# GpSimd in source order beside the attention, ScalarE and TensorE behind it, full rows in the middle slot, and a thinner last side slot

## The chip, the cores and the metric

The kernel runs on one core of a Trainium2 chip. Its engines are TensorE (PE in the profile, with its weight loads as PEld), VectorE (DVE), ScalarE (ACT), GpSimd (POOL) and SyncE (SP), whose queue issues most transfers; the indirect transfers (gathers and scatters by row index) are issued by GpSimd. Each engine takes its instructions strictly in the order in which the program has them, so one that waits holds everything behind it on that engine. The metric is the device time of one execution in microseconds.

## The reference

Attention over 8 batches, 8 heads, 576 positions and 64 dimensions, with a softmax that keeps only scores within `tau` of the row's maximum, and behind it a mixture of eight experts, of which each token takes one:

```
scores = scale * np.matmul(q, k.transpose(0, 1, 3, 2))
thresh = np.max(scores, axis=-1, keepdims=True) - tau
scores = np.where(scores >= thresh, scores, -1e9)
attn = softmax(scores);  x = attn @ v          # 4608 tokens of 512
logits = x @ w_gate + modality_bias[modality_id]
e_idx = np.argmax(logits, axis=1)              # top 1 of 8 experts
for e in range(E):
    h = np.maximum(x[mask] @ w1[e], 0.0)       # 512 -> 1024
    out[mask] = gate_w[mask, None] * (h @ w2[e])
```

All of it is in fp32. The kernel reaches that with operands split in two, a rounded high part and the rest as a low part (names with `h` and `l`), and three matmuls in place of one.

## The kernel before, in words

**The attention loop.** 32 pairs of heads, nine query tiles each, make 288 steps. A step does the scores (L369), their row maximum (VectorE, L386), the exponential (ScalarE, L392), mask and sum (VectorE, L404), transposes (L420) and the product with v (L458). Beside the steps of one pair the next is prepared by `prep_steps`: PE transposes k and q, ScalarE evacuates them as `str` (the last 64 positions) and `st` (the rest; L314), GpSimd splits them into high and low parts (`split_pool`, L282 and L283) `nk`, `qb` and `nq`, and SP then moves the parts to where the matmuls want them: `km<-nk` (L320) and `q<-nq` (L323), four transfers each. The first score tile of a pair reads `nk` and `qb`, the next ones `km` and `q`.

**The experts.** As soon as a batch is done, its tokens are routed. `route_a` and `route_b` rank them by expert (matmuls with the names `oh` and `ltri`), `posi` (L611) holds the rows, and five scatters (L617) write the table `tab` of token numbers, sorted by expert. A "slot" is a block of tokens of one expert (512, or 256 for the first two side slots). Seven side slots run beside the attention, one for each batch from the second on. A slot reads its piece of the table (`tb`, SP, L735), gathers its tokens (`xg`, GpSimd, L747, one for 128 tokens), transposes them (L761), and does both layers in pieces of three matmuls (L805 and L832). The weights arrive as `raw` (SP, L771 and L775; four buffers) and GpSimd splits them into `w1h`, `w1l`, `w2h`, `w2l` (L790, L792). The result `y` (VectorE, L845) is scattered to the output (GpSimd, L847). What a slot has to do besides matmuls are events with a due time in steps; its pieces wait in a queue, and each step takes some of them, spread so that the last side slot is done after `last` steps.

**The tail.** Behind the loop come the last batch's routing (`finish`, at XF = 301.5 steps), what is left of the last side slot, and from F0 = XF + 9.5 on the four slots that are always there (two of 512 tokens, one of 320, one of 256), whose high weight parts ScalarE splits off (L788). Conditional slots follow, which this data does not need.

**What sets the order.** `run_events` runs the events by their due time, which gives the order of the source. Engines named in `tc.manual_schedule(engines=...)` keep that order; the instructions of the others are ordered by a scheduler that works from modelled durations. Before, the loop has this for PE alone, and the tail for no engine.

Of the kernel before, what the change touches and what calls it, by code (L numbers as in the profile page):

```python
# [11 lines left out]
F32 = mybir.dt.float32  # L12
# [3 lines left out]
U32 = mybir.dt.uint32  # L16
# [3 lines left out]
ET = mybir.EngineType  # L20
# [9 lines left out]
def tile_attn_moe(  # L30
# [11 lines left out]
    out: bass.AP,  # L42
):

    C = {'prep': [0, 1, 2], 'tr0': 6, 'pv0': 7, 'tr1': 12, 'sums': 13, 'pv1': 13, 'x': 14, 'gate': [15, 16, 17, 18], 'route': 18, 'routeb': 21, 'E0': 28, 'L0': 4, 'pick': -14, 'vld': 6, 'qkld': -3, 'pre': 2.5, 'wl': 3.5, 'rows': -11, 'gat': [-9.5, -8.5, -5, -4], 'xt': [-6, -5, -2, -1], 'lc': 21, 't3': 84, 'neg': 1.0, 'draw': [2, 2, 2, 2, 1, 2, 2, 1, 2], 'last': 36, 'te': 8, 'warm': 24,
         'wS': [-6, -4.7, -3.4, 3, 12.5, 14, 15.5, 21.5, 4.2, 5.4, 6.6, 7.5, 22.7, 23.8, 24.9, 25.8],
         'wL': [-5.5, -4, -2.5, 2.7, 12, 13.3, 14.6, 21, 3.8, 4.9, 6, 7.1, 15.8, 22.2, 23.4, 24.6], 'ask': 4, 'exp': -12.5, 'two': 98, 'early': []}
    nc = tc.nc
# [2 lines left out]
    DM = H * D  # L51
    DF = w1.shape[2]
    N = B * S
    P = 128
# [8 lines left out]
    W = 512  # L63
# [498 lines left out]


    prev_scatter = []

    def route_a(b):
        lg = state.pop(("lg", b))
# [20 lines left out]
    def route_b(b):  # L588
        l, oh = state.pop(("route", b))
        shp = [P, NT, NE]  # L590

        rk = tbank()
        rkv = rk[:, 0:(NT + 1) * NE].rearrange("p (t e) -> p t e", e=NE)
        mm(rkv, ltri, oh, True, False)
        for t in range(NT):
            mm(rkv[:, t + 1:NT + 1, :], ones_bf, oh[:, t:t + 1, :].to_broadcast([P, NT - t, NE]),
               False, t == NT - 1)

        nc.scalar.activation(out=l, in_=l, func=AF.Exp)
        pos = small.tile([P, NT + 1, NE], F32, name="pos", bufs=1)  # L600
        nc.vector.tensor_tensor(out=pos, in0=rkv, in1=base.unsqueeze(1).to_broadcast([P, NT + 1, NE]),
                                op=ALU.add)
        nc.vector.tensor_copy(out=base, in_=pos[:, NT, :])
        nc.vector.tensor_tensor(out=pos[:, 0:NT, :], in0=pos[:, 0:NT, :],
                                in1=creg.unsqueeze(1).to_broadcast(shp), op=ALU.add)
        nc.vector.tensor_tensor(out=pos[:, 0:NT, :], in0=pos[:, 0:NT, :], in1=oh[:, 0:NT, :], op=ALU.mult)
        posi = small.tile([P, NT], I32, name="posi")
        posf = small.tile([P, NT], F32, name="posf", bufs=1)
        nc.vector.tensor_reduce(out=posf, in_=pos[:, 0:NT, :], axis=AX.X, op=ALU.add)
        nc.vector.memset(posf[0:P - R, NC:NT], float(TROWS))  # L610
        nc.vector.tensor_copy(out=posi, in_=posf)  # L611
        gs = small.tile([P, NT], F32, name="gs", bufs=1)
        nc.vector.tensor_reduce(out=gs, in_=l, axis=AX.X, op=ALU.add)
        nc.vector.tensor_scalar(out=gs, in0=gs, scalar1=1e-9, scalar2=None, op0=ALU.add)
        nc.vector.reciprocal(out=pay[:, b, :, 1].bitcast(F32), in_=gs)
        for t in range(NT):
            i = _inst(nc.gpsimd.indirect_dma_start(  # L617
                out=tab, out_offset=bass.IndirectOffsetOnAxis(ap=posi[:, t:t + 1].bitcast(U32), axis=0),
                in_=pay[:, b, t, :], in_offset=None, bounds_check=TROWS - 1, oob_is_err=False))
            for o in prev_scatter:  # L620
                tc.declare_no_dep(i, o, reason="every token has a row of its own")
            prev_scatter.append(i)
# [91 lines left out]
    def slot(where, group, nrow, WT=W, wq=lambda: wp, nbuf=(4, 3, 5), lo_eng=None, xq=None):  # L714
# [3 lines left out]
        box = {}  # L718
# [3 lines left out]
        def TP(t):  # L722

            return min(P, WT - t * P)
# [17 lines left out]
        def gather(t):  # L742
            def f():
                xg = xt_pool().tile([P, DM], F32, name="xg", bufs=nx[1])
                box[("xg", t)] = xg

                nc.gpsimd.indirect_dma_start(  # L747
                    out=xg[0:TP(t)], out_offset=None, in_=xs[0:nrow, :],
                    in_offset=bass.IndirectOffsetOnAxis(ap=box["tb"][0:TP(t), t, 0:1].bitcast(U32), axis=0),
                    bounds_check=nrow - 1, oob_is_err=False)  # L750
            return f

# [68 lines left out]
        def l2(g, t, z):  # L821
            def f():
                if z == 0:
                    box["ps"] = group()
                nt = TP(t)
                ps = box["ps"]
                ts = slice(t * P, (t + 1) * P)
                f_ = g * F2 + z
                hh, hl = box[("h", f_)]
                wh, wl = box[("w", 2, f_)]  # L830
                for y, (h, w) in enumerate(((hh, wh), (hh, wl), (hl, wh))):
                    nc.tensor.matmul(out=ps, lhsT=h[:, ts], rhs=w, start=(z == 0 and y == 0),  # L832
                                     stop=(z == F2 - 1 and y == 2))
                if z < F2 - 1:
                    return
                let_go(ps)
                ps = ps[0:nt]
                tb = box["tb"][0:nt]
                if g == 0:
                    y0 = xp.tile([P, DM], F32, name="y0", bufs=W // P)[0:nt]  # L840
                    nc.scalar.activation(out=y0, in_=ps, func=AF.Copy, scale=tb[:, t, 1:2].bitcast(F32))
                    box[("y0", t)] = y0
                    return
                y = xp.tile([P, DM], F32, name="y", bufs=2)[0:nt]
                nc.vector.scalar_tensor_tensor(out=y, in0=ps, scalar=tb[:, t, 1:2].bitcast(F32),  # L845
                                               in1=box.pop(("y0", t)), op0=ALU.mult, op1=ALU.add)
                i = _inst(nc.gpsimd.indirect_dma_start(  # L847
                    out=out, out_offset=bass.IndirectOffsetOnAxis(ap=tb[:, t, 0:1].bitcast(U32), axis=0),
                    in_=y, in_offset=None, bounds_check=N - 1, oob_is_err=False))
                for o in prev_out:  # L850
                    tc.declare_no_dep(i, o, reason="every token has a row of its own")
                prev_out.append(i)
            return f
# [48 lines left out]
    def at(t, f):  # L902
        events.setdefault(t, []).append(f)
# [118 lines left out]
        clear(fin["xp"], 4)  # L1022

    XF = NSTEP - NI + C['routeb'] + 1.5
    F0 = XF + 9.5
    at(XF, finish)

    def ask():
# [8 lines left out]
    def run_events(lo, hi):  # L1037
        while True:
            ts = [x for x in events if lo <= x < hi]
            if not ts:  # L1040
                return
            t = min(ts)
            for f in events.pop(t):
                f()

    LAG = 2
    with tc.manual_schedule(engines={ET.PE}):

        ps = tbank()
        for _ in range(C['warm']):  # L1050
# [1 line left out]
        prep_first(0)  # L1052
        for n in range(NSTEP + LAG):
            m = draw[n]
            if n == C['lc']:
                late_constants()
            if n == C['lc'] + 6:
# [32 lines left out]
            at(n + 0.01 * z, f)  # L1090
    for z, f in enumerate(work_q):
        at(NSTEP + LAG + z / 2, f)
    run_events(0, 10 ** 9)

    def more(cnt, j, z):
        if j < MAXN[z]:
# [39 lines left out]
```

## Time and profile before

| what | value |
|---|---|
| time, median of 3 runs | 1117.74 us (1115.88 to 1118.3) |
| time of the profiled execution | 1116.18 us |
| span of the profiled execution | 1114.5 us |
| PE busy | 1029.7 us, 92% of the span |
| VectorE, ScalarE, GpSimd busy | 725.7, 641.9, 537.9 us |
| mean granted TensorE clock | 0.976 of full speed |

In a group of the page stand the line, the engine, the operation, what it writes and reads, its count, then its busy time and the mean of one in ns, and the idle time of the engine just ahead of it with what ended most of it. In a row of an engine's timeline stand the start, the length, the instruction, and in brackets the idle time before it and what ended that. SPq is SP's queue, where a row is the issuing and not the transfer. A row of stretches gives the window, its length, then busy time and count for PE, PEld, DVE, ACT and POOL, the granted clock, the share of DMA, and GB/s.

### The profile page before, as it was taken

To read this page: it belongs to the slowest core of one execution; us is meant where nothing else is said; L and a number is where in the kernel's file an instruction comes from. 1 tells how busy PE (TensorE), PEld (TensorE's weight loads), DVE (VectorE), ACT (ScalarE), POOL (GpSimd) and SP (SyncE) were. 2 spreads that over 40 slices of the span, in tenths; PEclk is the share of its full clock that TensorE was granted. 3 is DMA by queue.
4 is the path that set the end of the run, shared out by engine and by line. 5 is a ranking of instruction groups with operands and counts; after the bars stand their busy time and mean duration, and the time that the engine had idled before them with its cause. 6 is when DMAs were issued, how large, how long until landed. Compare 5 with 4: busy or idle time off the path is not lost.

```text
span 1114.5 us, 20778 instructions
## 1 busy us (share of the span) xinstructions
PE 1029.7 (92%) x6683; PEld 809.9 (73%) x6683; DVE 725.7 (65%) x1773; ACT 641.9 (58%) x1474; POOL 537.9 (48%) x727
## 2 busy tenths in 40 slices
PE   7799869989798989999999999999999997999993
PEld 6676647777676767787777777777767775788883
DVE  6788857787568756876676766776677645243441
ACT  5687657666565656666666666566656523434440
POOL 2232345464655563665355644565265546442440
PEclk8999989999899999999999999999999999999997
DMA  5656557656666757476635763676465214644330
GB/s 123 140 136 160 124 128 184 165 110 165 165 161 130 180 129 184 102 202 162 168 82 141 197 161 91 148 206 147 107 141 152 97 39 134 216 145 131 131 99 21
DMA packets 212646, 156.06 MB, mean 140 GB/s; under 512 B 100782, under 2 KB 172462, under 8 KB 212528
## 3 DMA queue, kind: packets, MB, share of 16 engines
q1 hardware_dynamic: 205392, 135.72, 49.1%
q0 software_dynamic: 7136, 18.92, 5.2%
q8 instruction: 55, 0.90, 0.3%
q14 instruction: 63, 0.52, 0.1%
HBM read 84.12 MB, written 19.35 MB: 93 GB/s over the span
## 4 chain that ended last, share of the span: by engine, by line
PE 57%; DVE 3%; issue 2%; DMA 2%; ACT 1%; POOL 1%; another core or an unknown queue 0%; POOLq 0%; ACTq 0%; SPq 0%
PE bk L458 8%; PE bk L832 8%; PE bk L805 8%; PE s L369 8%; PE pm L832 7%; PE pm L805 6%; PE bk L420 6%; PE bk L761 1%; PE bk L311 1%; DVE pr L404 1%; PE bk L449 1%; DVE nm L386 1%; ACT e L392 1%; DMA xg<-xs,tb 1%; PE bk L507 1%
## 5 line engine op out<-in xcount | busy, mean ns | idle before, releaser
L386 DVE TENSOR_REDUCE nm<-s 128x1 f32<-128x576 f32 x288 | 216.9, 754 | 135.1 <-PE s L369 125.2
L392 ACT ACTIVATE e<-s,nm 128x576 f32<-128x576 f32 x288 | 215.0, 747 | 113.8 <-DVE nm L386 107.2
L404 DVE SCALAR_TENSOR_TENSOR pr<-s,nm,e 128x576 f32<-128x576 f32 x288 | 231.5, 815 | 75.1 <-ACT e L392 67.4
L369 PE MATMUL s<-km,q 128*128 128x288 f32 x1024 | 202.3, 320 | 41.1 <-DMA q<-nq 17.2
L431 ACT COPY ptm<-bk 128x512 f32<-128x512 f32 x256 | 149.3, 584 | 78.4 <-PE bk L420 66.4
L369 PEld LDWEIGHTS s<-km,q 128*128 128x128 f32 x1024 | 148.5, 192 | 62.1 <-issue 33.5
L420 PE MATMUL bk<-ident,pr 128*128 128x128 f32 x1152 | 175.8, 276 | 3.9 <-ACT ptm L431 2.0
L420 PEld LDWEIGHTS bk<-ident,pr 128*128 128x128 f32 x1152 | 143.6, 142 | 27.9 <-DVE hl L816 3.0
L458 PE MATMUL bk<-ptm,v_m 128*64 128x320 f32 (+1 forms) x1024 | 144.5, 420 | 0.1
L792 POOL TENSOR_TENSOR w2l<-raw,w2h 128x512 fp32r<-128x512 f32 x88 | 113.7, 1299 | 30.9 <-ACT w2h L788 26.7
L458 PEld LDWEIGHTS bk<-ptm,v_m 128*64 128x64 f32 x1024 | 67.6, 139 | 50.1 <-issue 10.3
L790 POOL CAST w2h<-raw 128x512 fp32r<-128x512 f32 x56 | 34.2, 613 | 140.1 <-DMA raw<-in_moe_w_dram 71.1
L433 ACT COPY rp<-pr 128x64 f32<-128x64 f32 x256 | 59.3, 248 | 56.5 <-DVE pr L404 47.0
L805 PE MATMUL bk<-xh,w1h 128*128 128x512 f32 (+1 forms) x212 | 85.5, 403 | 1.1 <-ACT xh L272 0.9
L805 PE MATMUL bk<-xl,w1h 128*128 128x512 f32 (+1 forms) x212 | 77.3, 365 | 1.9 <-DVE xl L273 1.9
L805 PE MATMUL bk<-xh,w1l 128*128 128x512 f32 (+1 forms) x212 | 76.9, 363 | 0.0
L747 POOL DMA_INDIRECT xg<-xs,tb x37 | 38.2, 1034 | 79.3 <-DMA tb<-tab 55.6
L832 PE MATMUL bk<-w2h,hh 128*128 128x512 f32 x176 | 75.7, 430 | 0.0
L847 POOL DMA_INDIRECT out_dram<-y,tb x37 | 38.6, 1042 | 74.4 <-DVE y L845 53.2
L792 POOL TENSOR_TENSOR w1l<-raw,w1h 128x512 fp32r<-128x512 f32 x56 | 71.8, 1285 | 2.9
L832 PE MATMUL bk<-w2h,hl 128*128 128x512 f32 x176 | 69.4, 394 | 0.0
L792 DVE TENSOR_TENSOR w1l<-raw,w1h 128x512 fp32r<-128x512 f32 x32 | 29.0, 908 | 61.5 <-ACT w1h L788 52.0
(205 smaller groups left out, 2006.7 us busy)
## 6 DMA issues: line engine op xcount, KB each, us to landing
raw<-in_moe_w_dram SPq DMA_DIRECT2D x176, 256.0 KB
q<-nq SPq DMA_DIRECT2D x124, 256.0 KB
km<-nk SPq DMA_DIRECT2D x124, 144.0 KB
v_m<-in_v_dram SPq DMA_DIRECT2D x32, 256.0 KB
xs<-xr SPq DMA_DIRECT2D x32, 256.0 KB
k_m<-in_k_dram SPq DMA_DIRECT2D x62, 128.0 KB
q_m<-in_q_dram SPq DMA_DIRECT2D x62, 128.0 KB
vr<-in_v_dram SPq DMA_DIRECT2D x64, 16.0 KB
```

The lines of the kernel that those rows point to most:

```text
L369: nc.tensor.matmul(out=sps[:, hf, 0:SH], lhsT=a, rhs=x, start=(z == 0), stop=(z == len(passes) - 1))
L386: in_line(nc.vector.tensor_reduce(out=nm[:, 0:1], in_=sv, axis=AX.XY, op=ALU.max, negate=True), two)
L392: nc.scalar.activation(out=e, in_=sv, func=AF.Exp, bias=nm[:, 0:1])
L404: in_line(nc.vector.scalar_tensor_tensor(out=pr.rearrange("p (a x) -> p a x", a=2), in0=s2[n % 2][:, :, 0:SH], scalar=nm[:, 1:2], in1=e, o ...
L420: nc.tensor.transpose(out=ps[:, kc * P:(kc + 1) * P], in_=pr[:, kc * P:(kc + 1) * P], identity=ident)
L431: nc.scalar.copy(out=ptm[:, s, :, (c % 2) * P:(c % 2 + 1) * P], in_=pv)
L433: nc.scalar.copy(out=rp[:, i, :], in_=pr[:, SA:S])
L458: nc.tensor.matmul(out=o, lhsT=lhsT, rhs=rhs, start=start, stop=stop, skip_group_check=True)
L792: eng.tensor_tensor(out=lo, in0=raw, in1=hi.bitcast(F32), op=ALU.subtract)
L805: nc.tensor.matmul(out=ps[:, 0:WT], lhsT=a[:, cs], rhs=x[:, c, :], start=(c == 0 and z == 0), stop=(c == KC - 1 and z == 2))
L832: nc.tensor.matmul(out=ps, lhsT=h[:, ts], rhs=w, start=(z == 0 and y == 0), stop=(z == F2 - 1 and y == 2))
L847: i = _inst(nc.gpsimd.indirect_dma_start(out=out, out_offset=bass.IndirectOffsetOnAxis(ap=tb[:, t, 0:1].bitcast(U32), axis=0), in_=y, in_o ...
```

## The change

Three edits, and two numbers that go with them.

- **Order.** In the loop GpSimd keeps the order of the source too, beside PE. In the tail ScalarE and PE keep it, where the scheduler ordered all engines.
- **Scatter.** The five table scatters are no longer issued inside `route_b` but by an event one step later (`'sc': 1`, function `scatter`), which puts them at a later place in the source order.
- **Full rows.** In the middle slot of 320 tokens the third tile has 64 tokens. Its gather, ScalarE's copy, VectorE's sum and the scatter now take all 128 partitions; the index rows behind the 64 point past the end and are dropped by the bounds check.
- **Numbers.** `last` goes from 36 to 50, so the last side slot's pieces are spread thinner and 57 of them are left for the tail where 53 were. F0 goes from XF + 9.5 to XF + 14.

```
-  'last': 36, 'te': 8, 'warm': 24,
+  'last': 50, 'te': 8, 'f0': 14, 'sc': 1, 'warm': 24,
...
+    step = [0]
...
         nc.vector.reciprocal(out=pay[:, b, :, 1].bitcast(F32), in_=gs)
+        at(step[0] + C['sc'], lambda: scatter(b, posi))
+
+    def scatter(b, posi):
         for t in range(NT):
             i = _inst(nc.gpsimd.indirect_dma_start(
                 out=tab, out_offset=bass.IndirectOffsetOnAxis(ap=posi[:, t:t + 1].bitcast(U32), axis=0),
...
-                    out=xg[0:TP(t)], out_offset=None, in_=xs[0:nrow, :],
-                    in_offset=bass.IndirectOffsetOnAxis(ap=box["tb"][0:TP(t), t, 0:1].bitcast(U32), axis=0),
+                    out=xg, out_offset=None, in_=xs[0:nrow, :],
+                    in_offset=bass.IndirectOffsetOnAxis(ap=box["tb"][:, t, 0:1].bitcast(U32), axis=0),
...
-                ps = ps[0:nt]
-                tb = box["tb"][0:nt]
+                tb = box["tb"]
...
-                    y0 = xp.tile([P, DM], F32, name="y0", bufs=W // P)[0:nt]
+                    y0 = xp.tile([P, DM], F32, name="y0", bufs=W // P)
...
-                y = xp.tile([P, DM], F32, name="y", bufs=2)[0:nt]
+                y = xp.tile([P, DM], F32, name="y", bufs=2)
...
-    F0 = XF + 9.5
+    F0 = XF + C['f0']
...
-    with tc.manual_schedule(engines={ET.PE}):
+    with tc.manual_schedule(engines={ET.PE, ET.Pool}):
...
+            step[0] = n
...
-    run_events(0, 10 ** 9)
+    with tc.manual_schedule(engines={ET.Activation, ET.PE}):
+        run_events(0, 10 ** 9)
```

Line numbers from L617 on grow by 4 and those behind the slot's second layer by 2 or 3: L747 is L751 after the change, L792 is L796, L847 is L849.

**The order on GpSimd, first side slot.** Behind the first table scatter of the run, before the change, from the split of the next pair's keys (`nk_152<-st`) to that of its queries (`nq<-st`). The slot's first gather stands ahead of these rows, right behind the five scatters.

```order
L282 CAST nk_152<-st 128x512
L790 CAST w1h<-raw 128x512
L283 TENSOR_TENSOR nk_152<-st,nk_152 128x512
L792 TENSOR_TENSOR w1l<-raw,w1h 128x512
L790 CAST w1h<-raw 128x512
L747 DMA xg<-xs,tb 128x512
L792 TENSOR_TENSOR w1l<-raw,w1h 128x512
L790 CAST w1h<-raw 128x512
L792 TENSOR_TENSOR w1l<-raw,w1h 128x512
L282 CAST nq<-st 128x512
L283 TENSOR_TENSOR nq<-st,nq 128x512
```

The same place after the change:

```order
L282 CAST nk_152<-st 128x512
L283 TENSOR_TENSOR nk_152<-st,nk_152 128x512
L282 CAST nq<-st 128x512
L283 TENSOR_TENSOR nq<-st,nq 128x512
L794 CAST w1h<-raw 128x512
L796 TENSOR_TENSOR w1l<-raw,w1h 128x512
L751 DMA xg<-xs,tb 128x512
L794 CAST w1h<-raw 128x512
L796 TENSOR_TENSOR w1l<-raw,w1h 128x512
L751 DMA xg<-xs,tb 128x512
```

The queries' split moved from behind both gathers and three weight splits to ahead of all of them.

**The order on SP, second side slot.** SP's row in the second side slot, some 140 us later, up to the transfers of the queries of one pair (`q_147`), before (an ISA row is a register instruction that goes with the load behind it):

```order
L775 DMA raw<-in_moe_w_dram 128x512
L771 ISA
L771 DMA raw<-in_moe_w_dram 128x4x128
L771 ISA
L771 DMA raw<-in_moe_w_dram 128x4x128
L113 DMA q_r<-in_q_dram 64x2x64
L113 DMA k_r<-in_k_dram 64x2x64
L771 ISA
L771 DMA raw<-in_moe_w_dram 128x4x128
L115 DMA k_m<-in_k_dram 128x4x64 x2
L320 DMA km_149<-nk_151 64x576 x4
L323 DMA q_147<-nq 64x2x512 x4
```

SP's row up to the same transfers after:

```order
L779 DMA raw<-in_moe_w_dram 128x512
L113 DMA q_r<-in_q_dram 64x2x64
L113 DMA k_r<-in_k_dram 64x2x64
L115 DMA k_m<-in_k_dram 128x4x64 x2
L320 DMA km_149<-nk_151 64x576 x4
L323 DMA q_147<-nq 64x2x512 x4
L779 ISA
L779 DMA raw<-in_moe_w_dram 128x512
```

The loads of w1 that stood ahead of `km` and `q` come later now, though SP's order is the scheduler's in both.

**The order on GpSimd at the handover.** Around the last batch's five scatters, before (`w2h`, `w2l` and the last `w1h`, `w1l` belong to the last side slot, the four gathers to the first slot of the tail):

```order
L790 CAST w2h<-raw 128x512
L792 TENSOR_TENSOR w2l<-raw,w2h 128x512
L790 CAST w2h<-raw 128x512 x2
L792 TENSOR_TENSOR w2l<-raw,w2h 128x512 x2
L617 DMA tab<-pay,posi 37888x2 x5
L790 CAST w1h<-raw 128x512
L792 TENSOR_TENSOR w1l<-raw,w1h 128x512
L747 DMA xg<-xs,tb 128x512 x4
```

The same place after:

```order
L794 CAST w2h<-raw 128x512
L621 DMA tab<-pay,posi 37888x2 x5
L796 TENSOR_TENSOR w2l<-raw,w2h 128x512
L794 CAST w2h<-raw 128x512 x2
L796 TENSOR_TENSOR w2l<-raw,w2h 128x512
L794 CAST w1h<-raw 128x512
L796 TENSOR_TENSOR w2l<-raw,w2h 128x512
L796 TENSOR_TENSOR w1l<-raw,w1h 128x512
L751 DMA xg<-xs,tb 128x512 x4
```

The scatters stand ahead of most of the w2 splits now, and the last w1 split behind them. On PE, 31 pieces stand between the ranking matmuls of the last batch and the first transposes of the tail's first slot (one and four of L832 that close the first half of the side slot, 16 of L805, ten of L832), where 22 stood (one of L832, 16 of L805, five of L832).

More of the change, by code (lines that the diff above doesn't have):

```diff
@@ L43, in tile_attn_moe @@
 ):
-    C = {'prep': [0, 1, 2], 'tr0': 6, 'pv0': 7, 'tr1': 12, 'sums': 13, 'pv1': 13, 'x': 14, 'gate': [15, 16, 17, 18], 'route': 18, 'routeb': 21, 'E0': 28, 'L0': 4, 'pick': -14, 'vld': 6, 'qkld': -3, 'pre': 2.5, 'wl': 3.5, 'rows': -11, 'gat': [-9.5, -8.5, -5, -4], 'xt': [-6, -5, -2, -1], 'lc': 21, 't3': 84, 'neg': 1.0, 'draw': [2, 2, 2, 2, 1, 2, 2, 1, 2], 'last': 36, 'te': 8, 'warm': 24,
+    C = {'prep': [0, 1, 2], 'tr0': 6, 'pv0': 7, 'tr1': 12, 'sums': 13, 'pv1': 13, 'x': 14, 'gate': [15, 16, 17, 18], 'route': 18, 'routeb': 21, 'E0': 28, 'L0': 4, 'pick': -14, 'vld': 6, 'qkld': -3, 'pre': 2.5, 'wl': 3.5, 'rows': -11, 'gat': [-9.5, -8.5, -5, -4], 'xt': [-6, -5, -2, -1], 'lc': 21, 't3': 84, 'neg': 1.0, 'draw': [2, 2, 2, 2, 1, 2, 2, 1, 2], 'last': 50, 'te': 8, 'f0': 14, 'sc': 1, 'warm': 24,
          'wS': [-6, -4.7, -3.4, 3, 12.5, 14, 15.5, 21.5, 4.2, 5.4, 6.6, 7.5, 22.7, 23.8, 24.9, 25.8],
@@ L824, in f @@
                     box["ps"] = group()
-                nt = TP(t)
                 ps = box["ps"]
```

## The prediction

> **What bounds the kernel now.** I read the page's busy times first, then its groups, then stretches of the run, then each engine's instructions in order of time around the holes.
>
> The page, parts 1 and 5:
>
> ```profile
> PE 1029.7 (92%) x6683; PEld 809.9 (73%) x6683; DVE 725.7 (65%) x1773; ACT 641.9 (58%) x1474; POOL 537.9 (48%) x727
> ...
> L369 PE MATMUL s<-km,q 128*128 128x288 f32 x1024 | 202.3, 320 | 41.1 <-DMA q<-nq 17.2
> ...
> L792 POOL TENSOR_TENSOR w2l<-raw,w2h 128x512 fp32r<-128x512 f32 x88 | 113.7, 1299 | 30.9 <-ACT w2h L788 26.7
> L790 POOL CAST w2h<-raw 128x512 fp32r<-128x512 f32 x56 | 34.2, 613 | 140.1 <-DMA raw<-in_moe_w_dram 71.1
> ...
> L747 POOL DMA_INDIRECT xg<-xs,tb x37 | 38.2, 1034 | 79.3 <-DMA tb<-tab 55.6
> ```
>
> PE is the bound, 1029.7 of 1114.5 us. So only holes in PE can be won. One releaser stands out: PE waits 17.2 us at L369 for q, a transfer that SP issues once GpSimd (POOL) has split it. GpSimd itself is only 48% busy, but it stands 55.6 us at gathers that wait for a table and 71.1 us at weight casts that wait for a load. Since it takes its instructions in order, whatever is behind such a wait is late too.
>
> PE in order of time, at the holes:
>
> ```profile
> 165.66 1.30 PE L369 MATMUL s<-km,q 128*128 128x288 f32 x4 [9.27 <-DMA q<-nq]
> ...
> 169.65 0.66 PE L761 MATMUL bk<-ident,xg 128*128 128x128 f32 x4
> ...
> 303.13 1.30 PE L369 MATMUL s<-km,q 128*128 128x288 f32 x4 [7.65 <-DMA q<-nq]
> ...
> 306.66 0.79 PE L369 MATMUL s<-km,q 128*128 128x288 f32 x4
> ...
> 417.16 0.77 PE L369 MATMUL s<-km,q 128*128 128x288 f32 x4 [3.17 <-issue]
> ```
>
> Two holes for q, 9.27 and 7.65 us, and one of 3.17 us at the same line. Behind the two long ones the matmuls are slow: four of L369 take 1.30 us, where the same four take 0.79 at 306.66. At 0.6 of full speed the stretches 165.66 to 169.65 (3.99 us) and 303.13 to 306.66 (3.53 us) hold about 1.6 and 1.4 us of loss.
>
> The last hole is where the loop hands over to the tail:
>
> ```profile
> 850.00:900.00 50.00, 48.78 (x311) 37.21 (x310) 30.50 (x71) 26.01 (x61) 20.19 (x22) 1.00 0.36 107
> 900.00:950.00 50.00, 42.17 (x197) 31.05 (x196) 25.37 (x76) 13.71 (x25) 30.52 (x32) 0.97 0.32 96
> 950.00:1000.00 50.00, 49.61 (x223) 39.70 (x222) 18.28 (x25) 21.19 (x36) 22.40 (x20) 1.00 0.59 178
> ```
>
> After the length of the stretch comes PE's busy time: nearly full before 900, then 7.8 us idle of 50, and nearly none behind 950. The rest of the tail holds nothing to win.
>
> **The change part by part.** *GpSimd in source order in the loop: the first hole.* GpSimd, with ACT's evacuation of q (L314) and SP's issue:
>
> ```profile
> 134.31 0.97 POOL L617 DMA_INDIRECT tab<-pay,posi  x1 [0.30 <-issue]
> 144.21 1.05 POOL L747 DMA_INDIRECT xg<-xs,tb  x1 [8.93 <-DMA tb<-tab]
> ...
> 148.80 0.24 POOL L282 CAST qb<-str 64x64 fp32r<-64x64 f32 x1 [3.11 <-DMA xg<-xs,tb]
> ...
> 158.69 0.61 POOL L282 CAST nq<-st 128x512 fp32r<-128x512 f32 x1
> 159.37 1.26 POOL L283 TENSOR_TENSOR nq<-st,nq 128x512 fp32r<-128x512 f32 x1
> ```
>
> ```profile
> 146.51 0.69 ACT L314 ACTIVATE st<-bk,gq 128x512 f32<-128x512 f32 x1
> ```
>
> ```profile
> 160.66 3.46 SPq L323 DMA_DIRECT2D q<-nq  x4
> ```
>
> Its source st was there at 147.2, the cast ran at 158.69: 11.5 us late, behind a gather that waited, three weight splits (613 + 1299 ns each) and a second gather. SP sent q 0.03 us after the split ended, so the queue of SP was not what held it. In source order nk and nq stand ahead of both gathers and of the weight splits. nq then runs straight behind st: 147.2 + 0.61 + 1.26 = 149.1. The four transfers take 3.46 us to issue, and the last was followed by PE 1.5 us after (165.66 - 164.12). So q is there at 149.1 + 3.46 + 1.5 = 154.1, or 2 us later if SP is still busy with km: between 154.1 and 156.1, and PE asks at 156.4. The hole goes: 9.27 + 1.6 = 10.9 us. What is late next are the gathers, now behind nq at about 151 and 154 where they were at 144.21 and 154.51. The L761 that uses the first stood at 169.65, without the 10.9 us at about 158.8; a gather took 3.5 us to land (144.21 + 1.05 to 148.80), so 155.6 for the first and 158.6 for the second. I charge 0.8 us, bounds 0 and 2.
>
> *The second hole.* The same three engines:
>
> ```profile
> 280.30 0.61 POOL L790 CAST w2h<-raw 128x512 fp32r<-128x512 f32 x1 [10.41 <-DMA raw<-in_moe_w_dram]
> ...
> 295.20 0.62 POOL L282 CAST nq<-st 128x512 fp32r<-128x512 f32 x1
> ```
>
> ```profile
> 280.33 0.69 ACT L314 ACTIVATE st<-bk,gq 128x512 f32<-128x512 f32 x1
> ```
>
> ```profile
> 286.27 6.91 SPq L771 DMA_DIRECT2D raw<-in_moe_w_dram  x2
> ...
> 298.29 3.42 SPq L323 DMA_DIRECT2D q<-nq  x4
> ```
>
> nq ran 14.2 us behind its source, with four w2 splits and a scatter ahead of it, and SP stood 6.91 us at weight loads that wait for GpSimd to free their buffers. After, nk, qb and nq of this pair stand ahead of the w2 splits, and in SP's row the loads on which it stood come behind q. So nq follows its source (done at 281.0) by 1.9 us, and q is there near 281.0 + 1.9 + 3.4 + 1.5 = 288, where PE asks at 295.5. Gone: 7.65 + 1.4 = 9.1 us, with 7 us of cover.
>
> *The third.*
>
> ```profile
> 394.51 0.70 ACT L314 ACTIVATE st<-bk,gq 128x512 f32<-128x512 f32 x1
> ```
>
> ```profile
> 410.27 0.61 POOL L282 CAST nq<-st 128x512 fp32r<-128x512 f32 x1
> ```
>
> A lag of 15.1 us, and PE started at 417.16. In source order one or two casts are ahead, and the 3.2 us go. Elsewhere q has enough slack (no other hole is put down to it), and the shorter lag is worth nothing.
>
> *The scatter one step later, and the handover.* In the loop a step is about 3.2 us (the 290 steps end at 913.83) and the code asks for the table four steps behind the scatter, some 12.6 us: nothing. At the handover:
>
> ```profile
> 913.83 0.47 PE L832 MATMUL bk<-w2h,hh 128*128 128x512 f32 x1
> ...
> 922.74 0.39 PE L805 MATMUL pm<-xh,w1l 128*128 128x512 f32 x1
> 925.43 0.50 PE L805 MATMUL pm<-xh,w1h 128*128 128x512 f32 x1 [2.30 <-issue]
> ...
> 926.79 0.50 PE L805 MATMUL pm<-xh,w1l 128*128 128x512 f32 x1 [0.63 <-POOL w1l L792]
> ...
> 928.12 0.63 PE L805 MATMUL pm<-xh,w1h 128*128 128x512 f32 x1
> ...
> 939.25 0.63 PE L761 MATMUL bk<-ident,xg 128*128 128x128 f32 x4 [2.55 <-DMA xg<-xs,tb]
> ```
>
> ```profile
> 914.40 1.27 POOL L790 CAST w2h<-raw 128x512 fp32r<-128x512 f32 x2
> ...
> 923.78 0.97 POOL L617 DMA_INDIRECT tab<-pay,posi  x1 [0.31 <-issue]
> 924.76 0.62 POOL L790 CAST w1h<-raw 128x512 fp32r<-128x512 f32 x1
> 925.47 1.27 POOL L792 TENSOR_TENSOR w1l<-raw,w1h 128x512 fp32r<-128x512 f32 x1
> ...
> 932.27 1.06 POOL L747 DMA_INDIRECT xg<-xs,tb  x1 [5.53 <-DMA tb<-tab]
> ```
>
> From the last routing matmul to the first transposed gather PE has 22 pieces (a piece is three matmuls; the 39th starts at 922.74, so 8.91 / 38 = 0.23 us from start to start and 0.70 us a piece): 15.3 us of work in 25.4, so 10.1 us lost. After, 31 pieces (21.6 us) stand there: four more were left over by the loop, five come forward from between and behind the gathers' transposes. The gathers' data at 939.25 is then no wait at all. But one wait grows: behind the five scatters GpSimd now has w2l, w2h, w2h, w2l before the last w1h, and w2l before its w1l. From 924.75 that is 1.30 + 1.27 + 1.30 + 0.62 = 929.2 for w1h and 931.8 for w1l; PE wants them after 17 pieces, at 913.83 + 11.8 = 925.7. So 3.5 us, and again 2.1 us for w1l, and the slow matmuls behind them: 0.63 instead of 0.39 us at 928.12, about 1.4 us over seven of them. That is 7.0 lost where 10.1 was: 3.1 us won; bounds 0 (GpSimd's row slips by 3 us) and 8 (the row fits in before the scatters).
>
> [...]
>
> *Four pieces fewer in the last six loop steps.* PE moves 2.8 us of work from there to the tail. If PE bounds these steps, nothing changes; if they run by softmax, 2.8 us of hole arises. Ends 0 and 2.8, I take 1.0, nearer to the first because PE was 48.78 of 50 us busy from 850 to 900, with VectorE at 30.50.
>
> *ScalarE in source order in the tail.* Before, a weight cast held a finished piece's relu; in source order the relu comes first. What that cost is inside the 10.1. A cast that waits for its load can now hold what follows: bounds 0 and 5; I take 1.
>
> *Full rows.* One gather, one ScalarE copy, one VectorE sum and one scatter grow from 64 to 128 partitions:
>
> ```profile
> 274.27 0.75 DVE L845 SCALAR_TENSOR_TENSOR y<-bk,tb,y 128x512 f32<-128x512 f32 x1
> ...
> 1078.01 0.74 DVE L845 SCALAR_TENSOR_TENSOR y<-pm,tb,y 64x512 f32<-64x512 f32 x1
> ```
>
> The sum takes the same on 64 and on 128 rows, and the engines are under half busy in that part (950 to 1000: VectorE 18.28, ScalarE 21.19, GpSimd 22.40 of 50). I take nothing, bounds -0.5 and 0.5.
>
> The sum: 10.9 - 0.8 + 9.1 + 3.2 + 3.1 - 1.0 - 1.0 = 23.5 us. The profiled execution took 1116.18 us, 1.56 below the median 1117.74; from the median, 1094.
>
> **The rivals.** *One hole comes back.* Even in source order SP may stand at weight loads until GpSimd frees a buffer, and GpSimd at weight casts until they land (71.1 us in all before). If one such knot falls ahead of a q, the price is one hole, 8 to 9 us: 1103. For it: the knot at 286.27 exists. Against it: GpSimd frees the buffers earlier when it doesn't stand 55.6 us at gathers, which in the new order have splits ahead of them instead.
>
> *Slower.* The waits of gathers for their table (55.6 us in seven) stay in the row, and in five of the later pairs one stands ahead of nk and nq. If the table still lands 8 us after GpSimd gets there, nq is late in each of them. It decides from a lag of about 13 us, where PE began to wait (11.5 to 15.1 us above); at five holes of 7.65 us the time is 1094 + 38 = 1132, and from three holes on it is no longer faster. Against it: three or four splits of 1.9 us (613 + 1299 ns) now follow the scatter, 6 to 8 us, and then the table is there.
>
> *Nothing happens.* The holes at L369 stay since something else sends q late: 1118. The 0.03 us between the split and SP's issue speaks against it.
>
> **How the numbers follow.** Forecast 0.64, one hole back 0.24, slower 0.08, nothing 0.04. The range takes in the second case and the bounds: low 1094 - 5 (handover 8) - 3 (the two charges of 1.0 and the 0.8 at nothing) = 1086; high 1103 + 2 (gathers) + 3 (handover nothing) = 1108. A change under 0.2% (2.2 us) cannot be told from none here: faster 0.88, same 0.04, slower 0.08.
>
> **What would show it.** Right: L369's wait for q near zero and no L369 of 1.30 us; nq within 3 us behind st everywhere; PE's first L761 of the tail without a wait, and a wait of 4 to 6 us at the last L805 group ahead of it. Wrong: a hole at L369 or L761 in 150 to 420, GpSimd standing at an xg gather with st already there, or ScalarE held by a cast in the tail while PE stands.

## Result and profile after: 1068.06 us, about twice the gain that was forecast

The changed kernel takes 1068.06 us (median of 4 runs, 1066.14 to 1068.77), the kernel before 1117.24 (4 runs, 1115.88 to 1118.30): a ratio of 0.9558, interval 0.9540 to 0.9576. The profiled execution took 1066.14 us, its span is 1064.4. Against the span before (1114.5) that is 50.1 us less, where 23.5 were forecast. The direction was right and the time lies outside the range (1086 to 1108).

The page of after: busy times, then the group of the score matmuls, with its idle time and what ended most of it.

```profile
PE 1019.6 (96%) x6683; PEld 805.1 (76%) x6683; DVE 714.5 (67%) x1773; ACT 638.7 (60%) x1474; POOL 541.6 (51%) x727
...
L369 PE MATMUL s<-km,q 128*128 128x288 f32 x1024 | 201.1, 318 | 19.4 <-DVE pr L404 14.3
```

PE has the same 6683 matmuls, is 10 us less busy (fewer of them run at the slow clock: 0.989 of full speed in the mean, 0.976 before), and is now 96% busy. L369's idle time went from 41.1 to 19.4 us, and what ends most of it is no longer q.

GpSimd at the place of the first hole, with ScalarE's evacuation and SP's issue:

```profile
147.44 0.61 POOL L282 CAST nq<-st 128x512 fp32r<-128x512 f32 x1 [1.10 <-ACT st L314]
148.13 1.28 POOL L283 TENSOR_TENSOR nq<-st,nq 128x512 fp32r<-128x512 f32 x1
...
151.48 1.07 POOL L751 DMA_INDIRECT xg<-xs,tb  x1
...
154.69 1.04 POOL L751 DMA_INDIRECT xg<-xs,tb  x1
```

```profile
146.69 0.69 ACT L314 ACTIVATE st<-bk,gq 128x512 f32<-128x512 f32 x1
```

```profile
149.45 3.89 SPq L323 DMA_DIRECT2D q<-nq  x4
```

nq now waits for its source and runs 0.1 us behind it, where it ran 11.5 us late. The gathers stand behind it, at 151.48 and 154.69, and no longer wait for their table.

The stretches around the handover to the tail (length, then busy time and count of PE, PEld, DVE, ACT, POOL, clock, DMA share, GB/s), then PE's waits there:

```profile
850.00:900.00 50.00, 47.50 (x248) 35.10 (x245) 20.21 (x78) 13.69 (x29) 31.34 (x35) 1.00 0.35 101
900.00:950.00 50.00, 49.09 (x223) 39.79 (x222) 20.02 (x26) 18.69 (x33) 19.72 (x18) 1.00 0.48 149
```

```profile
890.11 0.50 PE L809 MATMUL pm<-xh,w1h 128*128 128x512 f32 x1 [0.79 <-POOL w1h L794]
...
892.57 0.50 PE L809 MATMUL pm<-xh,w1l 128*128 128x512 f32 x1 [1.72 <-POOL w1l L796]
```

Before, the stretch from 900 had 42.17 us of PE; now the handover, which comes 37 us earlier, costs 2.5 us at these two rows, and the first gathered transposes of the tail start without a wait.

Where the 50.1 us went. The lines of the loop are worked out from the start of each pair's first score matmul (L369), the rest from the last ranking matmul (L458: 913.66 before, 877.05 after), PE's last matmul (1096.65, 1055.95), the end of VectorE's last sum (1097.84, 1057.13) and the span.

```
place                                        forecast   measured
pair 6 to 7 (first hole, less the gathers)     10.1       10.0
pair 8 to 9                                     -          5.2
pairs 9 to 12 (second hole)                     9.1        8.6
pair 15 to 16 (third hole)                      3.2        3.4
pairs 20, 24 and 28 to the next                 -          6.2
other steps of the loop                         -          0.1
loop's end, four pieces moved out (2.8 us)     -1.0       +0.3
handover and tail (ScalarE's order in it)      +2.1       +6.9
behind VectorE's last sum                       0          9.4
sum                                            23.5       50.1
```

(Loop's end: 3.1 us shorter, of which 2.8 is work that went to the tail. Handover and tail: 4.1 us shorter with that 2.8 us more in it.) So the three holes for q came out within 0.5 us of the forecast, and 28.1 us came from places to which it gave 1.1. The 6.2 us of pairs 20, 24 and 28 come from delays that not every execution has (Controls, below).

### The profile page after: what moved, and what is told of

Read it like the earlier page. It is cut to its first block, busy times and chain, and to the rows that moved or that the text cites. A ratio compares the mean times of both kernels' runs of the same rounds, so it can differ in the third digit from the quotient of the medians.

```text
span 1064.4 us, 20773 instructions
## 1 busy us (share of the span) xinstructions
PE 1019.6 (96%) x6683; PEld 805.1 (76%) x6683; DVE 714.5 (67%) x1773; ACT 638.7 (60%) x1474; POOL 541.6 (51%) x727
## 4 chain that ended last, share of the span: by engine, by line
PE 83%; DVE 8%; issue 3%; ACT 2%; DMA 2%; POOL 1%; SPq 0%; another core or an unknown queue 0%; POOLq 0%; DVEq 0%; ACTq 0%
PE s L369 16%; PE bk L458 14%; PE bk L809 11%; PE bk L420 11%; PE bk L835 11%; PE pm L835 7%; PE pm L809 6%; DVE pr L404 3%; DVE nm L386 2%; PE bk L311 2%; PE bk L449 2%; PE bk L765 1%; PE bk L507 1%; PE bk L539 1%; ACT e L392 1%
## 5 line engine op out<-in xcount | busy, mean ns | idle before, releaser
L369 PE MATMUL s<-km,q 128*128 128x288 f32 x1024 | 201.1, 318 | 19.4 <-DVE pr L404 14.3
L369 PEld LDWEIGHTS s<-km,q 128*128 128x128 f32 x1024 | 147.7, 191 | 40.0 <-DVE pr L404 23.3
L458 PE MATMUL bk<-ptm,v_m 128*64 128x320 f32 (+1 forms) x1024 | 142.8, 416 | 0.1
L796 POOL TENSOR_TENSOR w2l<-raw,w2h 128x512 fp32r<-128x512 f32 x88 | 113.3, 1290 | 51.9 <-ACT w2h L792 45.9
L282 POOL CAST nk<-str 128x64 fp32r<-128x64 f32 x31 | 7.5, 242 | 237.4 <-ACT str L298 223.8
L458 PEld LDWEIGHTS bk<-ptm,v_m 128*64 128x64 f32 x1024 | 67.0, 137 | 49.3 <-issue 9.1
L849 POOL DMA_INDIRECT out_dram<-y,tb x37 | 38.4, 1038 | 89.8 <-DVE y L847 73.1
L796 POOL TENSOR_TENSOR w1l<-raw,w1h 128x512 fp32r<-128x512 f32 x56 | 71.7, 1280 | 4.4
L835 PE MATMUL bk<-w2l,hh 128*128 128x512 f32 x176 | 69.0, 392 | 0.0
L389 DVE TENSOR_SCALAR nm<-nm,ntau 128x1 f32<-128x1 f32 (+1 forms) x240 | 58.4, 243 | 5.6
```

Of the source, the lines that this page charges most:

```text
L369: nc.tensor.matmul(out=sps[:, hf, 0:SH], lhsT=a, rhs=x, start=(z == 0), stop=(z == len(passes) - 1))
L389: in_line(nc.vector.tensor_scalar(out=nm2[:, 1, o], in0=nm2[:, 0, o], scalar1=-1.0, scalar2=ntau, op0=ALU.mult, op1=ALU.add), two)
L458: nc.tensor.matmul(out=o, lhsT=lhsT, rhs=rhs, start=start, stop=stop, skip_group_check=True)
L796: eng.tensor_tensor(out=lo, in0=raw, in1=hi.bitcast(F32), op=ALU.subtract)
```

## Experiments

Each is timed against runs of the kernel before on the same chip, and those medians were 1109.22, 1110.99, 1115.02 and 1116.53 us in the four sets. So ratios are compared. "Closing" is the time from the end of VectorE's last sum to the end of the span, 16.6 us before and 7.3 after.

**Full rows alone.** The kernel before with the full rows' lines only:

```
-                    out=xg[0:TP(t)], out_offset=None, in_=xs[0:nrow, :],
-                    in_offset=bass.IndirectOffsetOnAxis(ap=box["tb"][0:TP(t), t, 0:1].bitcast(U32), axis=0),
+                    out=xg, out_offset=None, in_=xs[0:nrow, :],
+                    in_offset=bass.IndirectOffsetOnAxis(ap=box["tb"][:, t, 0:1].bitcast(U32), axis=0),
...
-                ps = ps[0:nt]
-                tb = box["tb"][0:nt]
+                tb = box["tb"]
```

> The kernel before with the full rows alone. Behind the last VectorE sum the kernel before still ran 16.6 us (1097.84 to 1114.5), the changed one 7.3 (1057.13 to 1064.4), and the difference is GpSimd's closing: a drain of 9.38 us against 0.72 and a semaphore step of 2.47 against 0.35. Theory A: the gather and the scatter on 64 partitions cause the long closing; then this kernel is 9 to 11 us faster than before, near 1107, with the whole gain behind the last sum. Rival B: the order in the tail causes it; then this kernel is within 1 us of before.

Measured: 1101.90 us against 1109.22, ratio 0.9928 (0.9905 to 0.9950), closing 7.45 us. So this edit, which was costed at nothing, is worth 7.3 us (the interval says 5.5 to 10.5), and its trace is 9.2 us shorter behind the last sum.

**The change without full rows.** The reverse of these lines, in the changed kernel.

> The changed kernel with 64 partitions in the middle slot's third tile, as before. Theory A (full rows shorten the closing): about 9 to 11 us slower than the changed kernel, near 1078, with GpSimd's drain back at some 9 us. Rival B (order): within 1 us of the changed kernel, near 1068.

Measured: 1073.45 us, ratio 0.9689 (0.9659 to 0.9719) where the changed kernel has 0.9558, closing 16.53 us. The last rows of GpSimd's timeline before, after, and of the full rows alone; the spans end at 1114.5, 1064.4 and 1100.1:

```profile
1098.12 0.98 POOL L847 DMA_INDIRECT out_dram<-y,tb  x1 [1.80 <-DVE y L845]
```

```profile
1058.88 0.99 POOL L849 DMA_INDIRECT out_dram<-y,tb  x1 [3.29 <-issue]
```

```profile
1094.42 0.99 POOL L845 DMA_INDIRECT out_dram<-y,tb  x1 [3.29 <-issue]
```

From the end of this last scatter to the end of the span it is 15.4 us before, 4.5 after, and 4.7 with the full rows alone. The timeline shows nothing there; the trace's own list of instructions has two of GpSimd in it that tell these kernels apart:

```
                    semaphore instruction   drain
64-row scatter            2.47 us           9.38 us
128-row scatter           0.35 us           0.72 us
```

**A 64-row scatter alone.** The changed kernel, with one of the full-row transfers short again: only the scatter of the middle slot's third tile.

```
-                    out=out, out_offset=bass.IndirectOffsetOnAxis(ap=tb[:, t, 0:1].bitcast(U32), axis=0),
-                    in_=y, in_offset=None, bounds_check=N - 1, oob_is_err=False))
+                    out=out, out_offset=bass.IndirectOffsetOnAxis(ap=tb[0:TP(t), t, 0:1].bitcast(U32), axis=0),
+                    in_=y[0:TP(t)], in_offset=None, bounds_check=N - 1, oob_is_err=False))
```

> The changed kernel with the middle slot's last output scatter on 64 partitions, its gather and sums on 128. With both short the closing behind the last VectorE sum took 16.5 to 16.7 us, with both full 7.3 to 7.6. Theory A: the short scatter makes it long: 16.6 us, drain 9.38. Rival B: the short gather does: 7.4 us, drain 0.72.

Measured: one run, 1076.24 us; closing 16.55 us, with the drain of 9.38. So it is the scatter on 64 partitions, the third from the end and 18 to 19 us ahead of the last one, that lengthens the end, and not the gather or the sum. Every kernel of this study with the short scatter closed in 16.5 to 16.7 us, every one with the full one in 7.3 to 8.0. Why a drain takes so much longer behind it stays open.

**GpSimd's order in the loop alone.** The kernel before with

```
-    with tc.manual_schedule(engines={ET.PE}):
+    with tc.manual_schedule(engines={ET.PE, ET.Pool}):
```

> The kernel before with GpSimd in source order in the loop alone; the scatter stays where it was in the code, the tail and the numbers as before. Theory: the loop's gain is this edit, the three waits for q (22 us as forecast) and the 11 us at the routing of batches, where VectorE's small instructions are shorter when GpSimd does not split weights beside them. So about 33 us faster, near 1084. Rival: half of the 11 us comes from the scatter's later place, then near 1090; or the scatter in the code's own place now holds GpSimd until the ranks are there, and the splits of the next pair behind it are late: then near 1100.

Measured: 1078.80 us against 1109.22, ratio 0.9722 (0.9694 to 0.9750): 30.4 us from one line. The time from one pair's first score matmul to the next one's, in this set:

```
pair              6-7    8-9    11-12  12-13  13-14  14-15  15-16
full rows only   32.18  27.08  34.56  25.96  24.60  31.99  33.86
loop order only  22.33  22.00  25.17  23.87  29.44  29.28  29.56
```

Besides the three holes for q, pair 8 to 9 gives 5.1 us here too, so that gain belongs to GpSimd's order. The order also costs something: from pair 13 to 14 it takes 4.8 us more, since PE stands for a gather that now has splits ahead of it, and slow matmuls follow (in the trace of the change itself this pair took 24.62 us):

```profile
348.63 1.00 PE L761 MATMUL bk<-ident,xg 128*128 128x128 f32 x4 [2.57 <-DMA xg<-xs,tb]
```

**The changed kernel with GpSimd scheduled in the loop.** The same line undone in the changed kernel.

> The changed kernel with GpSimd ordered by the scheduler in the loop, as before. Theory: it gives back the loop's part, 30 to 36 us, near 1100. Rival: the scatter's later event alone already moves GpSimd's order, so that only half returns, near 1085.

Measured: 1096.71 us, ratio 0.9887 (0.9856 to 0.9918). The holes are back (31.70 us from pair 6 to 7, 27.37 from 8 to 9, 34.21 from 11 to 12); the tail stays as good as in the changed kernel (178.94 us from the last ranking matmul to the last matmul, against 178.90). So loop and tail are separate gains.

**What the 5 us at pair 8 to 9 are.** Before, PE stood 3.85 us for ScalarE, which stood 3.83 us for VectorE's nm (the negative row maximum):

```profile
238.13 0.69 PE L449 MATMUL bk<-ident,rp 128*128 128x128 f32 x2 [3.85 <-ACT ptm L431]
```

```profile
236.86 0.74 ACT L392 ACTIVATE e<-s,nm 128x576 f32<-128x576 f32 x1 [3.83 <-DVE nm L386]
```

nm started at 236.02, right behind the small instructions of the routing (the pk rows, 1 x 8 elements). These, with GpSimd at the same time:

```profile
231.12 0.84 DVE L630 SCALAR_TENSOR_TENSOR pk_a<-pk_a,iota 1x8 f32<-1x8 f32 x1
...
231.90 0.62 DVE L611 CAST posi<-posf 128x5 int32<-128x5 f32 x1
...
232.61 1.26 DVE L633 TENSOR_SCALAR pk_a<-iota,pk_r 1x8 f32<-1x8 f32 x1
...
233.91 0.52 DVE L635 TENSOR_TENSOR pk_d<-pk_a,done 1x8 f32<-1x8 f32 x1
...
234.55 1.22 DVE L637 SCALAR_TENSOR_TENSOR done<-pk_a,done 1x8 f32<-1x8 f32 x1
```

```profile
230.66 1.29 POOL L283 TENSOR_TENSOR nk<-st,nk 128x512 fp32r<-128x512 f32 x1
231.89 0.61 POOL L282 CAST nq<-st 128x512 fp32r<-128x512 f32 x1
232.58 1.28 POOL L283 TENSOR_TENSOR nq<-st,nq 128x512 fp32r<-128x512 f32 x1
233.79 0.62 POOL L790 CAST w1h<-raw 128x512 fp32r<-128x512 f32 x1
234.49 1.26 POOL L792 TENSOR_TENSOR w1l<-raw,w1h 128x512 fp32r<-128x512 f32 x1
```

Read the ends: 231.96 beside 231.95, 232.52 beside 232.50, 233.87 beside 233.86, 234.43 beside 234.41, 235.77 beside 235.75. Each of these five VectorE instructions ends when the GpSimd instruction that was running ends, 0.01 to 0.02 us later. The ranking and picking of a batch is 19 small instructions (`pos` to `pk_i`). In the loop before, 16 of them take 0.45 us or more, and all 16 end 0.01 to 0.06 us behind a GpSimd cast or split. The trace shows the ends together, not what holds VectorE until then. After, GpSimd stands at a scatter or waits when most of this chain runs, and the same two instructions are short:

```profile
222.00 0.22 DVE L637 TENSOR_SCALAR pk_a<-iota,pk_r 1x8 f32<-1x8 f32 x1
...
222.53 0.14 DVE L641 SCALAR_TENSOR_TENSOR done<-pk_a,done 1x8 f32<-1x8 f32 x1
```

From the start of the first reduction of the chain (before 232.44, after 221.82) to nm (236.02, 222.90) it is 3.58 us before and 1.08 after, 2.5 us less. PE's wait of 3.85 us shrinks to 0.53, and from there to the next pair it takes 1.98 us instead of 3.32, with no slow matmuls: 4.7 of the 5.2 us. Six such long instructions of the ranking are left in the loop. VectorE's threshold (L389, 128 x 2) is as often long as before: 10 of 240 over 0.45 us, and 9 before. So source order took the collisions off this chain and did not abolish them.

**Keeping GpSimd busy beside the ranking.** Two kernels put the delay back into the changed kernel. Each adds a copy by ScalarE and GpSimd subtractions whose result nobody uses, ahead of the ranking of the batches but the last: ten of 96 columns (0.42 us each), and five of 320 (0.78 us each), some 4 us in all both times.

```
+        if b < B - 1:
+            busy = small.tile([P, 2, 96], F32, name="busy", bufs=1)
+            nc.scalar.copy(out=busy[:, 0, :], in_=rk[:, 0:96])
+            for _ in range(10):
+                nc.gpsimd.tensor_tensor(out=busy[:, 1, :], in0=busy[:, 0, :], in1=busy[:, 0, :], op=ALU.subtract)
```

> The changed kernel with ten small subtractions of 96 elements on GpSimd in seven of the eight routings, started by the ranks, so that they run beside VectorE's small instructions of the ranking and picking. They add about 4 us of GpSimd time to a routing and write nothing that is used. Theory: VectorE's small instructions take longer beside GpSimd's, their sum in a routing goes from 3.0 to 4.4 us to 5 to 6.5, and TensorE has new holes there: 3 to 12 us slower than the changed kernel. Rival: VectorE's small instructions keep their time, the scatter is 4 us later and nothing waits for it: within 2 us of the changed kernel.

> The changed kernel with five subtractions of 320 elements on GpSimd in seven of the eight routings, started by the ranks, each about 0.8 us long, where ten of 96 elements (0.42 us each, 4.2 us in all) moved VectorE's small instructions little. Theory: a small instruction of VectorE waits for the end of the GpSimd instruction that runs, so long ones cost more than many short ones: the sum of the small ones in a routing rises to 5 us or more, and TensorE gets new holes, 2 to 10 us slower than the changed kernel. Rival: it is GpSimd's busy time that counts, then the same as with the short ones, 3.1 to 3.9 us.

Measured: 1068.23 us, ratio 0.9572 (0.9514 to 0.9630), and 1069.90, ratio 0.9568 (0.9521 to 0.9614). With the short pieces 3 instructions of the ranking take 0.45 us or more, none of them beside a piece; with the long ones it is 17, of which 14 end with a piece. The 19 of a ranking sum to 3.1 to 3.8 us with the short ones and to 3.9 to 5.2 with the long ones: what counts is how long the GpSimd instruction is that one runs into. But neither kernel is measurably slower than the changed one. The long delays here come to at most 1.7 us in one ranking (each counted from 0.17 us), where before 4.4 us of them fell into the one at 228 to 236, ahead of an nm that PE needed. So the delay of VectorE is shown, instruction by instruction, and at pair 8 to 9 it is on the chain that held PE. The loss there was not brought back by these two kernels, and that the delay costs time elsewhere is not shown.

**ScalarE's order in the tail alone.** The kernel before with

```
-    run_events(0, 10 ** 9)
+    with tc.manual_schedule(engines={ET.Activation, ET.PE}):
+        run_events(0, 10 ** 9)
```

> The kernel before with ScalarE and TensorE in source order in the tail alone. Theory: the relu no longer stands behind weight casts that wait for a load, 1 to 4 us faster, near 1115, closing as long as before (A) or 9 us shorter (B), then near 1105. Rival: ScalarE in source order is held by casts that wait, slower by 1 to 5 us.

Measured: 1110.43 us, ratio 0.9999 (0.9977 to 1.0022): nothing.

**The two numbers alone.** The kernel before with `'last': 50` and `F0 = XF + 14`.

> The kernel before with the two numbers alone (last 50, F0 = XF + 14). Theory: more of the last side slot's work covers the wait for the table at the handover; 4 to 7 us faster, near 1112. Rival: without ScalarE's and GpSimd's order the added work waits for the last weight split and nothing is won, within 2 us of before.

Measured: 1111.73 us, ratio 1.0013 (0.9994 to 1.0032): nothing again. But what it gives and what it takes are both large. PE stands nowhere for the gathers in the tail, and then this, PE and ScalarE:

```profile
926.91 0.80 PE L832 MATMUL pm<-w2h,hh 128*128 128x512 f32 x1 [3.94 <-ACT hh L815]
```

```profile
919.83 1.14 ACT L788 CAST w1h<-raw 128x512 fp32r<-128x512 f32 x2 [8.01 <-DMA raw<-in_moe_w_dram]
...
925.11 0.62 ACT L788 CAST w1h<-raw 128x512 fp32r<-128x512 f32 x1 [2.11 <-DMA raw<-in_moe_w_dram]
```

ScalarE stood 8 us at a weight cast for a load, with the relu of finished pieces behind it. From the last ranking matmul to the last matmul it is 189.98 us, 7 more than before, of which 2.8 are the pieces that were moved there.

**Numbers and tail order together.**

> The kernel before with the two numbers and ScalarE in source order in the tail, together; each alone measured nothing. Theory: the added work at the handover is only won if the relu stands ahead of the weight casts that wait 8 us for their loads; together 6 to 10 us faster than before, with 179 to 181 us from the last ranks to the last matmul, where the numbers alone took 190.0 and the order alone 183.3. Rival: the gain of the changed kernel's handover comes from GpSimd's order in the loop; then within 2 us of before.

Measured: 1109.88 us against 1116.53, ratio 0.9931 (0.9908 to 0.9954), 178.83 us from the last ranking matmul to the last. Neither edit is worth anything alone, both together 6.7 us: with the old numbers relu held by casts isn't on PE's path, with the new ones it is, for 11 us (189.98 less 178.83).

**The change with the old numbers**, 36 and 9.5:

> The changed kernel with last 36 and F0 = XF + 9.5 again. Theory: the handover loses what the four pieces and the five that come ahead of the transposes covered, 3 to 7 us slower than the changed kernel, near 1073. Rival: with the order in the loop the table comes so early that nothing has to be covered: within 2 us of the changed kernel.

Measured: 1069.18 us, ratio 0.9631 (0.9595 to 0.9668), 182.26 us from ranking to the end. PE and VectorE there:

```profile
886.98 0.50 PE L809 MATMUL pm<-xh,w1h 128*128 128x512 f32 x1 [2.28 <-POOL w1h L794]
...
899.39 1.09 PE L765 MATMUL bk<-ident,xg 128*128 128x128 f32 x4 [4.97 <-DMA xg<-xs,tb]
```

```profile
877.35 2.48 DVE L662 SCALAR_TENSOR_TENSOR th<-th_lo,left 1x72 f32<-1x72 f32 x2
```

The wait for the gathers is back, and the numbers do more than fill it. With the old ones GpSimd's w2 splits get their buffer 1.2 us ahead of the last ranking matmul (before: 912.48 and 913.66), and th, 2.48 us for two, lasts as long as they do (before: to 918.26, the splits to 918.18); with the new ones 1.9 us behind it (after: 878.92 and 877.05), and th takes 0.37:

```profile
878.46 0.37 DVE L662 SCALAR_TENSOR_TENSOR th<-th_lo,left 1x72 f32<-1x72 f32 x2
```

```profile
879.68 1.01 POOL L621 DMA_INDIRECT tab<-pay,posi  x1 [0.15 <-DVE off L670]
```

So the scatters start 2.6 us behind the ranking, where they started 5.0 behind it (918.62). In all six traces with the old numbers th took 2.48 or 2.49 us, in all eleven with the new ones 0.36 or 0.37.

**The scatter at once.** `scatter(b, posi)` inside `route_b`, as before, with the rest of the change.

> The changed kernel with the five scatters issued inside the second half of the routing again, not one step later. Theory: in source order GpSimd now stands at the scatter until the ranks are there and the weight splits behind it are a few us late; nothing on TensorE waits for that: within 2 us of the changed kernel. Rival: the picking of experts on VectorE runs while GpSimd splits again or a split is late for TensorE: 5 to 12 us slower.

Measured: 1063.11 us, ratio 0.9566 (0.9533 to 0.9600): the same as the change. The later place of the scatter is worth nothing either way.

**SP in source order too.** `engines={ET.PE, ET.Pool, ET.SP}` in the loop of the changed kernel.

> The changed kernel with SyncE in source order in the loop as well. Theory: what is left of the waits for q at the first pairs with experts (the pair behind the first table took 22 to 25 us where its neighbours take 21) comes from SyncE's order, and 1 to 3 us go. Rival: in source order SyncE stands at a weight load or a table while q is ready behind it: 5 us slower or more.

Measured: 1102.43 us, ratio 0.9877 (0.9819 to 0.9936), 36 us worse than the change. PE's waits, summed by what ended them (us in total, times, longest):

```profile
PE bk L294 <- DMA q_r<-in_q_dram: 28.0, 10, 5.6
```

In the changed kernel that wait is 1.6 us in all. SP waits most in this kernel at the transfers of km, for GpSimd's nk, with those loads behind them in its row; in the changed kernel that wait is 13.9 us:

```profile
SPq L320 <- POOL nk L282: 164.0, 28, 11.8
```

SP's source order puts loads behind transfers that wait; source order is no good in itself, and was for GpSimd.

**Controls.** The changed kernel again, and the kernel before again:

> The changed kernel once more, beside the kernels of this call. Theory: 45 to 50 us faster than before on this chip too, ratio 0.955 to 0.960.

> The kernel before once more, for a second profile. In the first one three late holes (1.1, 1.2 and 4.0 us in the stretches of three pairs behind a routing) were not forecast. Theory A: they belong to the kernel and show again. Rival B: they belong to that execution; here the same pairs take 28.9 and 27.7 us instead of 30.4, 30.7 and 31.5, and the loop ends some 6 us sooner.

Measured: 1066.34 us, ratio 0.9562 (0.9506 to 0.9618); and 1119.87 in one run. The second has the same holes at q and most of the small ones, as theory A had it, and from pair 14 to 15 it took 33.62 us, where the first execution took 29.29. Times from three pairs to the next:

```
pair                          20-21  24-25  28-29
kernel before                 30.44  30.65  31.50
kernel before again           30.67  30.68  29.84
full rows alone               28.87  28.87  27.70
tail order alone              28.87  28.87  27.68
the change                    29.38  29.50  27.48
the change without full rows  28.87  28.86  27.47
```

Up to 860 us every engine takes the same instructions in the same order in the first four of these traces, and so it does in the last two. So the order of the loop does not decide whether these delays come, and where they are absent the change gains 0.2 us in the three places together, not 6.2. The change has such a place of its own: pair 12 to 13 took 28.60 us, and 23.88 in the same order without full rows. Chip 11 ran kernels with and without these delays, so they do not go with the chip. Their cause stays open, and so does whether the change makes them shorter where they come. At the largest of them in the kernel before, ScalarE and VectorE stop together, at 824 us, for a releaser that the profile calls remote; the trace has both waiting for a semaphore that only PE's instructions update, and its updates pause from 820.03 to 824.31. So what came late there were PE's own signals:

```profile
824.34 0.59 ACT L431 COPY ptm<-bk 128x512 f32<-128x512 f32 x1 [3.37 <-remote]
```

```profile
824.42 0.29 DVE L523 TENSOR_TENSOR xr<-bk,ri 128x128 f32<-128x128 f32 x1 [2.47 <-remote]
```

## Why the prediction fell short, step by step

**The three holes for q: right.** 10.0, 8.6 and 3.4 us for 10.1, 9.1 and 3.2, in the way that was told: nq at most 2.6 us behind its source in all 31 pairs (up to 15.1 before), no L369 of 1.30 us behind the start-up, and no gather that waits for its table (one wait over 2 us is left, 6.02, for PE; ten before, seven of them for the table). The rivals by which a hole comes back, or gathers hold nq in the later pairs, did not happen, and as was said against them, splits stand between scatter and gather: 12 to 20 casts and splits in the loop after, none or two before. That the first hole came within 0.1 us is luck. The 0.8 us charged there for late gathers did not arise; PE stood instead for q_r, the next pair's queries as SP loads them, which it never did before and which the forecast left out:

```profile
161.28 0.24 PE L294 MATMUL bk<-ident,q_r 64*128 64x64 f32 x1 [1.61 <-DMA q_r<-in_q_dram]
```

In the same order without full rows that wait was 2.41 us, slow matmuls followed, and pair 6 to 7 took 24.99 us where it took 21.77 here.

**What the loop also gave: not in the sum.** Pair 8 to 9, 5.2 us. The step that failed is the reading of the holes: only those ended by q were counted. The row of 238.13 was in the trace of before, and what ended it (ptm, nm, the pk rows, then GpSimd's splits) goes back in three steps to an instruction on 1 x 8 elements that takes 1.26 us. GpSimd's order was costed only through what waits for GpSimd's results, not through what runs beside it. The 6.2 us of the three small places hang on delays that come in some executions and not in others, whatever the order.

**Handover: the mechanism right, the size wrong.** Forecast were waits of 3.5 for w1h and 2.1 for w1l and 1.4 us of slow matmuls, 7.0 in all. Measured were 0.79 and 1.72, 2.5 together, and no slow matmul. The failed step is "From 924.75": the scatters' end was carried over from the old trace, 11.1 us behind the ranking, though 2.3 us of it were VectorE's th beside GpSimd's splits, which the new numbers move away. Two waits shorter than forecast by 3.1 and the clock's 1.4 make 4.5; with the 3.1 that stood in the sum that is 7.6, where 6.9 came, ScalarE's order included.

**Four pieces fewer in the loop: −1.0, measured +0.3.** PE bounds these steps, which the row of 48.78 busy of 50 had said; the charge should have been nothing.

**ScalarE's order: −1.0, measured nothing alone.** The guess was a loss. With the new numbers it is the condition of their gain, 11 us from the last ranking matmul to the end. The sum treated the edits as independent.

**Full rows: 0 with bounds of ±0.5, measured 7.3 alone and 9.4 in the two traces.** This is the largest single miss. The working looked at the engines beside the moved rows, where indeed nothing changes, and never at the 15.4 us between the end of the last instruction shown and the end of the span. They are in the first trace, a loss of 1.4% that no row explains, and the sentence "the rest of the tail holds nothing to win" was written without them. An end that no row explains cannot be given a bound of ±0.5.

**The scatter's step: nothing, as forecast.**

The range missed for the same two reasons: its low end, 1086, was made of the known terms' bounds. The unforeseen 5.2 and 9.4 alone reach below it.

## What to carry to other kernels

Before costing a change of order, look for small instructions that are far too long, and compare their ends with those of the neighbour engine: here an instruction on 8 elements lasted as long as GpSimd's split (1.26 and 1.28 us), and putting GpSimd in order moved that away from the critical chain. Account for the span to its end, the stretch behind the last row too: it was 15.4 us and hung on the shape of one transfer. When edits come together, ask of each whether another makes the wait that it removes: two that are worth nothing alone gave 6.7 us together.

## What the hardware showed

- An indirect scatter on 64 partitions near the end made GpSimd's closing drain 9.38 us long; on 128, with the 64 rows too many pointing past the end, 0.72.
- A small VectorE instruction that runs into a GpSimd cast or split can last until that one ends: beside splits of 1.3 us two of them took 1.22 and 1.26 us, after the change 0.14 and 0.22.
- The same idle time of PE does not always bring the slow clock: behind a wait of 2.28 us and 0.62 or 0.63 more, the next matmul took 0.80 us with tail order alone and 0.50 with the old numbers; the granted clock was 0.70 there (921 to 926) and 1.00 (886 to 890). Before, 3.17 us of idle time at 417.16 brought no slow matmul (clock 1.00 from there to 421). What decides it is not shown.

```profile
923.63 0.80 PE L805 MATMUL pm<-xh,w1l 128*128 128x512 f32 x1 [0.62 <-POOL w1l L792]
```

```profile
888.34 0.50 PE L809 MATMUL pm<-xh,w1l 128*128 128x512 f32 x1 [0.63 <-POOL w1l L796]
```
